# Float16 pairs for every second group of four heads in a sigmoid attention with a gated layer

## The chip, the core and the metric

One core of one Trainium2 chip runs the whole program in one launch. The metric is the device time of an execution in microseconds (us); three executions of the kernel before took 1127.08, 1126.84 and 1126.88 us, median 1126.88. Five engines work beside each other, each through its own instructions in order, and wait for one another by semaphores: TensorE (PE, with its weight loads as PEld), VectorE (DVE), ScalarE (ACT), GpSimd (POOL) and SyncE (SP), whose queue starts nearly all transfers.

## The reference

The inputs are q, k and v of 8 batches, 12 heads, 448 positions and 64 numbers a head, and three weights, all float32 by value.

```
scores = scale * np.matmul(q, k.transpose(0, 1, 3, 2)) - np.log(S)
attn = 1.0 / (1.0 + np.exp(-scores))
attn_out = np.matmul(attn, v)
x = attn_out.transpose(0, 2, 1, 3).reshape(B * S, H * D)        # 3584 x 768
gate = 1.0 / (1.0 + np.exp(-(x @ w_gate)))                      # w_gate, w_val: 768 x 1536
return gate * (x @ w_val) @ w_out                               # w_out: 1536 x 768
```

The attention has no sum over keys: each score goes through a sigmoid of its own. The weights reach the chip as 64-bit floating-point words and are converted there.

## The kernel before, in words

The program has an attention stage and a stage of layers. The layers (`product`, `unit`, `first_layers`, `c_visit`) form every product as sums of float16 pairs: a matrix is split into a high and a low float16 part, and three products (low x high, high x high, high x low) are added up in PSUM. L659 issues them all. So their operands have to be split by the chip first: `convert` does it for the weights, `split_x` for x.

**The attention stage.** Its loop (from L584) goes over 24 groups m, each of four heads of one batch (two pairs p of two heads h), and in each group over 7 beats g. A beat takes 64 keys of all four heads or, in the slots of this version, 128 keys of one pair with one mixed slot in the middle (g = 3). `scores(m, g)` forms four float32 products of 64 x 64 by 64 x 448 on four quarters of the array (L502) into one of two PSUM tiles `sc`, then ScalarE takes the sigmoid of all 896 columns (L510). Two beats later (`LAG`) `values` multiplies with v (L527) and adds up in PSUM tiles `av`. A pair of heads has two such sums, so `finish` copies one (L537) and `finish_adds` adds the other by VectorE (L544), and the result x goes to DRAM.

**Beside the beats.** After the TensorE work of a beat the loop issues a share of other work, in an order that is written out by hand; every engine keeps to that order. The generator `convert` is stepped so that its first `n_chunks` = 58 steps are spread evenly over beats 0 to 146 and the rest up to beat 168 (`BESIDE`). Two steps convert a chunk of 128 x 384 words: `begin` takes the magnitude (L214), `limit` clamps it by GpSimd (L195), `first` makes a power of two with the sign (L201, L202), `second` makes the mantissa and multiplies (L209, L210, L211); then the largest is found (L107). After four chunks the scale of a block of weights is formed from its maximum over all partitions. For that the maximum of each partition goes as `each` through TensorE (L508, into free columns of `sc`), and ScalarE copies what all partitions told (L513); this is what the text calls a telling. L126 and L120 to L123 then form the scale as powers of two (`powers`). GpSimd adds blocks (L259) and makes the high parts (L377), VectorE the low parts (L229), and SP stores them. From group 7 on the x of the first two batches is loaded back, its maxima are taken, and it is split too (L385 for the low parts).

**The start.** `load_first` brings q and k of the first pair, then v, then the second pair, then four tiles of words; `load_qk(m + 1)` loads the next group at g = 0 of the one before, in one of two buffers.

Of the kernel before, what the change touches and what calls it, by code (L numbers as in the profile page):

```python
# [20 lines left out]
P = 128  # L21
# [9 lines left out]
BESIDE = 146, 168  # L31

AHEAD, AHEAD_FF = 4, 3
# [22 lines left out]
def sigmoid_attention_glu_kernel(ctx: ExitStack, tc: tile.TileContext, qk, v, wg, wv, wo, out):  # L56
# [111 lines left out]
    class Words:  # L168
# [28 lines left out]
        def first(self):  # L197
# [3 lines left out]
            nc.vector.tensor_scalar(out=e, in0=e, scalar1=3, scalar2=0x3F800000, op0=ALU.logical_shift_left, op1=ALU.bitwise_and)  # L201
            nc.vector.scalar_tensor_tensor(out=e, in0=raw[:, :, 1], scalar=0xC0000000, in1=e, op0=ALU.bitwise_and, op1=ALU.bitwise_or)  # L202

        def second(self):

            raw, f = self.begun.pop(0)
            self.spent += 1
            m = self.pool.tile([P, CW], U32, tag="wm", name="wm", bufs=1)
            nc.vector.tensor_scalar(out=m, in0=raw[:, :, 1], scalar1=11, scalar2=0x80000000, op0=ALU.logical_shift_left, op1=ALU.bitwise_or)  # L209
            nc.vector.scalar_tensor_tensor(out=m, in0=raw[:, :, 0], scalar=21, in1=m, op0=ALU.logical_shift_right, op1=ALU.bitwise_or)  # L210
            nc.vector.scalar_tensor_tensor(out=f, in0=m, scalar=2.0 ** -31, in1=f, op0=ALU.mult, op1=ALU.mult)  # L211
# [266 lines left out]
    with tc.manual_schedule(), tc.tile_pool(name="att", bufs=2) as att, tc.tile_pool(name="sc", bufs=2, space=PSUM) as scp, \  # L478
            tc.tile_pool(name="av", bufs=1, space=PSUM) as avp:
        loads, avs, pending, adds, stores = {}, {}, [], [], []  # L480

        def load_qk(m):

            if m < B * NQ:
                loads[m] = [att.tile([P, 2, 2 * S], F32, tag="qk", name="qk")]
                nc.sync.dma_start(out=loads[m][0], in_=qk[m // NQ, m % NQ])

        def load_v(m):
            if m < B * NQ:
                loads[m].append(att.tile([P, 7, 2, D], F32, tag="v", name="v"))  # L490
                nc.sync.dma_start(out=loads[m][1], in_=v[m // NQ, m % NQ])

        def scores(m, g):


            qkt = loads[m][0]
            sc = scp.tile([P, 2, 512], F32, tag="sc", name="sc")
            for h in range(2):
                for u in range(2):
                    p = u if g == 3 else g // 4  # L500
                    k0 = S + (3 * P if g == 3 else g % 4 * P + u * HP)
                    nc.tensor.matmul(sc[halves[u], h, :S], lhsT=qkt[halves[h], p, k0:k0 + HP], rhs=qkt[halves[h], p, :S],  # L502
                                     start=True, stop=True)
            told = spreads[:1]
            for sp in told:
                spreads.remove(sp)
                for h in range(2):
                    nc.tensor.matmul(sc[:, h, S:], lhsT=sp.each, rhs=ident[:, halves[h]], start=True, stop=True)  # L508
# [556 lines left out]
```

## Time and profile before

| | us |
|---|---|
| median of three runs | 1126.88 |
| the profiled execution, as timed | 1127.14 |
| its span, first to last instruction | 1125.4 |
| first product of the layers starts at | 261.92 |
| busy in the span: PE, DVE, ACT, POOL | 1119.5, 790.4, 672.2, 496.9 |

The profile is of one execution; its granted TensorE clock is 0.999 of full speed. A row of a group has the line, the engine, the operation, the tile written and the tiles read, the shape and the count; behind the first bar the busy time in us and the mean of one in ns; behind the second the idle time of the engine ahead of these instructions and what ended it. A row in order of time begins with its start and its length in us. A row of a table of stretches has the length, then busy time and count for PE, PEld, DVE, ACT and POOL, then the granted clock, the busy share of the transfer engines and GB/s. Each float32 product shows as two weight loads and two products.

### The profile page before, as it was taken

The numbers are of one execution on the slowest core, as the hardware profiler recorded it, in microseconds if no ns is written. First come the engines' busy times: TensorE is split into PE (matmuls) and PEld (weight loads), VectorE is DVE, ScalarE is ACT, GpSimd is POOL, SyncE is SP. The second block draws the span as 40 slices with busy tenths as digits, with TensorE's granted clock in tenths as the row PEclk, the third lists the DMA queues.
The fourth block names the chain that finished last, engine by engine and source line by source line (L and its number), as shares of the span: only waits on it lengthen the run. The fifth ranks groups of instructions, "written<-read, shape, count | busy, mean of one in ns | idle before, by whom it ended". The sixth has DMA issues, their size and how long they took to land.

```text
span 1125.4 us, 20712 instructions
## 1 busy us (share of the span) xinstructions
PE 1119.5 (99%) x7269; PEld 554.4 (49%) x7269; DVE 790.4 (70%) x1318; ACT 672.2 (60%) x1265; POOL 496.9 (44%) x424
## 2 busy tenths in 40 slices
PE   9999999999999999999999999999999999999998
PEld 4444434445555555555555555555555555555554
DVE  3578989974574555667678887887348687676863
ACT  6777778876775765766565756666444444253430
POOL 0045778791252332253233443333365294572940
PEclk9999999999999999999999999999999999999999
DMA  7679979888687746753566798979756876867644
GB/s 254 233 245 326 320 251 316 302 281 303 241 274 254 254 144 213 265 163 104 151 216 207 236 355 256 322 235 256 223 167 200 252 225 206 277 199 247 190 127 140
DMA packets 174536, 265.30 MB, mean 236 GB/s; under 512 B 49248, under 2 KB 151392, under 8 KB 174432
## 3 DMA queue, kind: packets, MB, share of 16 engines
q1 hardware_dynamic: 174144, 263.80, 72.6%
q8 instruction: 57, 0.93, 0.3%
q14 instruction: 47, 0.39, 0.1%
q10 hardware_dynamic: 288, 0.18, 0.1%
HBM read 182.48 MB, written 81.43 MB: 235 GB/s over the span
## 4 chain that ended last, share of the span: by engine, by line
PE 99%; ACT 0%; DVE 0%; DVEq 0%; issue 0%
PE un L659 76%; PE av L527 11%; PE sc L502 11%; PE sc L565 0%; PE sc L508 0%; ACT a L510 0%; PE un L627 0%; DVE g L944 0%; DVEq L1060 0%; DVE bias L79 0%; DVEq L944 0%
## 5 line engine op out<-in xcount | busy, mean ns | idle before, releaser
L659 PEld LDWEIGHTS <-A 128*128 128x128 f16 x3024 | 295.5, 98 | 275.8 <-issue 0.7
L659 PE MATMUL un<-b,A 128*128 128x448 f16 x1512 | 296.6, 352 | 0.0
L659 PE MATMUL un<-b,v 128*128 128x448 f16 x1512 | 296.3, 352 | 0.0
L659 PE MATMUL un<-hh,A 128*128 128x448 f16 x1008 | 273.0, 352 | 0.0
L659 PEld LDWEIGHTS <-v 128*128 128x128 f16 x1512 | 147.8, 98 | 137.7
L510 ACT ACTIVATE a<-sc,bias 128x896 f32<-128x896 f32 x168 | 169.5, 1010 | 62.4 <-PE sc L502 54.5
L659 PE MATMUL un<-hl,A 128*128 128x448 f16 x504 | 177.6, 352 | 0.0
L527 PE MATMUL av<-a,v 64*64 64x448 f32 x1344 | 166.5, 537 | 0.0
L502 PE MATMUL sc<-qk 64*64 64x448 f32 x1344 | 165.8, 537 | 0.4 <-ACT a L510 0.4
L869 POOL TENSOR_TENSOR g<-c,g 128x448 f32<-128x448 f32 x44 | 59.1, 1344 | 184.9 <-DVE c L642 98.2
L195 POOL TENSOR_SCALAR wf<-wf 128x384 f32<-128x384 f32 x72 | 41.9, 582 | 204.3 <-ACT wf L217 131.8
L854 ACT ACTIVATE g<-c,back 128x448 f32<-128x448 f32 x72 | 48.2, 670 | 77.6 <-DVE c L642 75.1
L502 PEld LDWEIGHTS sc<-qk 64*64 64x64 f32 x1344 | 56.1, 133 | 74.7 <-issue 59.5
L642 DVE TENSOR_TENSOR c<-un,u 128x448 f32<-128x448 f32 x72 | 44.8, 622 | 66.6 <-PE un L659 58.3
L527 PEld LDWEIGHTS av<-a,v 64*64 64x64 f32 x1344 | 56.0, 133 | 68.9 <-issue 64.8
L259 POOL TENSOR_TENSOR wf<-wf 128x384 f32<-128x384 f32 x72 | 82.7, 1154 | 13.2 <-DVE whl L229 12.2
L345 POOL TENSOR_TENSOR v<-v 128x448 f32<-128x448 f32 x48 | 64.0, 1362 | 51.6 <-DVE hl L385 50.6
L345 POOL TENSOR_TENSOR b<-b 128x448 f32<-128x448 f32 x48 | 67.5, 1442 | 40.6 <-DVE hl L385 40.6
L675 ACT COPY p<-un 128x448 f32<-128x448 f32 x48 | 25.6, 533 | 57.9 <-PE un L659 57.6
L345 POOL TENSOR_TENSOR r<-r 128x448 f32<-128x448 f32 x36 | 46.5, 1306 | 24.2 <-DVE b L385 23.8
L544 DVE TENSOR_TENSOR x<-av,x 128x448 f32<-128x448 f32 x48 | 29.8, 620 | 38.8 <-ACT x L537 37.6
L104 ACT ACTIVATE junk<-g 128x448 bf16<-128x448 f32 x88 | 50.7, 576 | 7.4 <-POOL g L869 5.9
(348 smaller groups left out, 1361.2 us busy)
## 6 DMA issues: line engine op xcount, KB each, us to landing
A<-ad SPq DMA_DIRECT2D x168, 192.0 KB, 3.3
A<-oo SPq DMA_DIRECT2D x168, 192.0 KB, 2.6
qk<-qk SPq DMA_DIRECT2D x23, 896.0 KB, 5.5
h<-g SPq DMA_DIRECT2D x88, 224.0 KB, 3.4
ad<-whl SPq DMA_DIRECT2D x84, 192.0 KB, 4.1
bd<-b SPq DMA_DIRECT2D x30, 448.0 KB, 3.5
b<-bd SPq DMA_DIRECT2D x30, 448.0 KB, 5.8
v<-vv SPq DMA_DIRECT2D x24, 448.0 KB, 5.1
```

The source lines that it names most:

```text
L104: nc.scalar.activation(junk[:, :x.shape[-1]], x, AF.Abs, accum_out=to)
L195: nc.gpsimd.tensor_scalar(out=f, in0=f, scalar1=F32_MAX, scalar2=F64_ZERO, op0=ALU.min, op1=ALU.max)
L259: nc.gpsimd.tensor_tensor(out=x, in0=y, in1=z, op=op)
L345: engine.tensor_tensor(out=to, in0=x, in1=y, op=ALU.subtract)
L502: nc.tensor.matmul(sc[halves[u], h, :S], lhsT=qkt[halves[h], p, k0:k0 + HP], rhs=qkt[halves[h], p, :S], start=True, stop=True)
L510: nc.scalar.activation(a, sc[:, :, :S], AF.Sigmoid, bias=bias, scale=scale)
L527: nc.tensor.matmul(avs[key][halves[h], :S], lhsT=vt[halves[u], g, h], rhs=a[halves[u], h], start=start, stop=g == last)
L544: nc.vector.tensor_tensor(out=x, in0=other, in1=x, op=ALU.add)
L642: engine.tensor_tensor(out=to, in0=x, in1=y, op=ALU.add)
L659: nc.tensor.matmul(acc, lhsT=w, rhs=m, start=begin and i == 0, stop=i == len(terms) - 1, skip_group_check=not begin)
L854: nc.scalar.activation(gates[i], acc, AF.Sigmoid, scale=of_unit[0])
L869: nc.gpsimd.tensor_tensor(out=h, in0=acc, in1=gates[i], op=ALU.mult)
```

## The change

**Slots.** Every beat now takes 64 keys of all four heads: quarter (h, p) of the array works for head h of pair p in `scores` and in `values` alike. A pair of heads has one sum, `av` is kept twice, the adds by VectorE are gone, and ScalarE copies the two sums of a group in the second and third beat of the next (`finish_copy`).

**Float16 pairs.** In groups with odd m the scores are three rounds of four float16 products (low k x high q, high k x low q, high x high) with separate weight loads. `split_qk(m + 1)` makes the parts during group m, one step a beat: at g = 0 the largest magnitudes of q and of k in each partition (one reduction of 1792 elements, L499, and L501); behind the scores of g = 2 TensorE sums them over the partitions (four products of two columns, L545), ScalarE copies the sums behind that beat's sigmoid (L556); at g = 3 VectorE forms the powers and the two high parts (L509 to L515); at g = 4 and g = 5 the low parts of q and of k (L518). In group 0 all of this is one beat later. The powers undone go into the sigmoid as its scale. The buffer for both parts is one, that for q and k is three, and `load_qk(m + 2)` loads two groups ahead.

**Tellings** now use quarters of the array (L551) in place of the whole.

**Conversion.** `first` and `second` put sign, exponent and mantissa together by shifts and masks, three operations in place of five, also for the weights that are converted beside the layers. Its pace is 58% of the steps up to beat 77 and the rest up to beat 150; three tiles of words are loaded ahead, not four. Loading, subtracting and splitting x start up to three groups earlier.

```
-            nc.vector.tensor_scalar(out=e, in0=e, scalar1=3, scalar2=0x3F800000, op0=ALU.logical_shift_left, op1=ALU.bitwise_and)
+            nc.vector.tensor_scalar(out=e, in0=e, scalar1=3, scalar2=0x3FFFFFFF, op0=ALU.logical_shift_left, op1=ALU.bitwise_and)
...
-            m = self.pool.tile([P, CW], U32, tag="wm", name="wm", bufs=1)
-            nc.vector.tensor_scalar(out=m, in0=raw[:, :, 1], scalar1=11, scalar2=0x80000000, op0=ALU.logical_shift_left, op1=ALU.bitwise_or)
-            nc.vector.scalar_tensor_tensor(out=m, in0=raw[:, :, 0], scalar=21, in1=m, op0=ALU.logical_shift_right, op1=ALU.bitwise_or)
-            nc.vector.scalar_tensor_tensor(out=f, in0=m, scalar=2.0 ** -31, in1=f, op0=ALU.mult, op1=ALU.mult)
+            e = f.bitcast(U32)
+            nc.vector.scalar_tensor_tensor(out=e, in0=raw[:, :, 0], scalar=29, in1=e, op0=ALU.logical_shift_right, op1=ALU.bitwise_or)
...
-BESIDE = 146, 168
-AHEAD, AHEAD_FF = 4, 3
+PACE = (0, 0), (77, 0.58), (150, 1)
+AHEAD, AHEAD_FF = 3, 3
...
+        def split_qk(m):
+            if m >= B * NQ or not in_halves(m):
+                return
+            x = loads[m]
+            each = att.tile([P, 2], F32, tag="qkm", name="qkm", bufs=1)
+            told = att.tile([P, 2], BF16, tag="qkt", name="qkt", bufs=1)
+            nc.vector.tensor_reduce(out=each, in_=x.rearrange("r p t s -> r t p s"), axis=AX.XY, op=ALU.max,
+                                    apply_absolute_value=True)
+            nc.vector.tensor_scalar(out=told, in0=each, scalar1=SUM_MAX, scalar2=TINY, op0=ALU.min, op1=ALU.max)
+            yield
+            total = att.tile([P, 2, 2], F32, tag="qka", name="qka", bufs=1)
+            qk_sums.append((told, total))
+            yield
+            yield
...
+            nc.vector.tensor_tensor(out=m_, in0=total[:, 0], in1=total[:, 1], op=ALU.add)
+            powers(m_, s_, inv)
+            nc.vector.tensor_scalar(out=back, in0=inv[:, 0:1], scalar1=inv[:, 1:2], scalar2=scale, op0=ALU.mult, op1=ALU.mult)
+            hl = att.tile([P, 2, 2, 2, S], F16, tag="hl", name="hl", bufs=1)
+            parts[m] = hl, back
+            for t in range(2):
+                nc.vector.tensor_scalar(out=hl[:, 0, t], in0=x[:, :, t], scalar1=s_[:, t:t + 1], scalar2=None, op0=ALU.mult)
+            yield
+            for t in range(2):
+                nc.vector.scalar_tensor_tensor(out=hl[:, 1, t], in0=x[:, :, t], scalar=s_[:, t:t + 1], in1=hl[:, 0, t],
+                                               op0=ALU.mult, op1=ALU.subtract)
+                yield
...
+            for i, (kt, qt) in enumerate(((1, 0), (0, 1), (0, 0)) if in_halves(m) else ((None, None),)):
+                for h in range(2):
+                    for p in range(2):
+                        qs, ks_ = (x[halves[h], qt, 0, p], x[halves[h], kt, 1, p, ks]) if in_halves(m) else \
+                            (x[halves[h], p, 0], x[halves[h], p, 1, ks])
+                        nc.tensor.matmul(sc[halves[p], h, :S], lhsT=ks_, rhs=qs, start=i == 0, stop=i == 2 or not in_halves(m))
...
+            for p, queue in enumerate((nc.sync, nc.scalar)):
+                queue.dma_start(out=first[:, p, :S + P], in_=qk[0, 0][:, p, :S + P])
+            for p in range(2):
+                nc.sync.dma_start(out=first[:, p, S + P:], in_=qk[0, 0][:, p, S + P:])
+            load_qk(1)
+            load_v(0)
```

**TensorE where a group opens.** Before, around the opening of group 2 (the load of its q and k is the transfer waited for; `a` is the sigmoid's result):

```order
L527 MATMUL av<-a,v 64x448 x4
L502 MATMUL sc<-qk 64x448 [waits DMAHW3_49,Activation_49]
L502 MATMUL sc<-qk 64x448 x3
L527 MATMUL av<-a,v 64x448 x4
L502 MATMUL sc<-qk 64x448 [waits Activation_49]
```

Now, the opening of group 3, the second with float16 parts (`hl` holds them):

```order
L539 MATMUL sc<-qk 64x448 [waits Activation_49]
L539 MATMUL sc<-qk 64x448 x3
L569 MATMUL av<-a,v 64x448 x4
L539 LDWEIGHTS hl [waits DVE_49]
L539 MATMUL sc<-hl 64x448 [waits Activation_49]
L539 LDWEIGHTS hl
L539 MATMUL sc<-hl 64x448
```

The first scores of such a group wait for VectorE, and their weight loads stand as instructions of their own.

**VectorE between the beats.** Before, in the conversion (`whl` holds parts of the weights, `wm` the mantissas):

```order
L229 SCALAR_TENSOR_TENSOR whl<-wf,w00s,whl 128x384 [waits Pool_49]
L107 TENSOR_REDUCE w01c<-wf 128x1 [waits DVE_49]
L214 TENSOR_SCALAR wf<-wraw 128x384 [waits DMAHW1_49]
L201 TENSOR_SCALAR wf<-wf 128x384 [waits Pool_49]
L202 SCALAR_TENSOR_TENSOR wf<-wraw,wf 128x384 [waits DVE_49]
L229 SCALAR_TENSOR_TENSOR whl<-wf,w00s,whl 128x384 [waits Pool_49]
L209 TENSOR_SCALAR wm<-wraw 128x384
L210 SCALAR_TENSOR_TENSOR wm<-wraw,wm 128x384 [waits DVE_49]
L211 SCALAR_TENSOR_TENSOR wf<-wm,wf 128x384 [waits DVE_49]
```

Now, the parts of group 15, made during group 14, from the high parts to the second low part:

```order
L515 TENSOR_SCALAR hl<-qk,qk_2561 128x896 [waits PE_49]
L515 TENSOR_SCALAR hl<-qk,qk_2561 128x896
L518 SCALAR_TENSOR_TENSOR hl<-qk,qk_2561,hl 128x896 [waits DVE_49]
L229 SCALAR_TENSOR_TENSOR whl<-wf,w11s,whl 128x384 [waits DMAHW3_49,Pool_49]
L109 TENSOR_REDUCE w20c<-wf 128x1
L214 TENSOR_SCALAR wf<-wraw 128x384 [waits DMAHW1_49]
L203 TENSOR_SCALAR wf<-wf 128x384 [waits Pool_49]
L204 SCALAR_TENSOR_TENSOR wf<-wraw,wf 128x384 [waits DVE_49]
L518 SCALAR_TENSOR_TENSOR hl<-qk,qk_2561,hl 128x896
```

Five steps of the conversion (L203 and L204 are the former L201 and L202, L109 the former L107) stand between the two low parts. What stands there differs from group to group.

**VectorE at the start.** Before, its first work:

```order
L214 TENSOR_SCALAR wf<-wraw 128x384 [waits DMAHW5_49]
L214 TENSOR_SCALAR wf<-wraw 128x384 [waits DMAHW6_49]
L201 TENSOR_SCALAR wf<-wf 128x384 [waits Pool_49]
L202 SCALAR_TENSOR_TENSOR wf<-wraw,wf 128x384 [waits DVE_49]
L544 TENSOR_TENSOR x<-av,x 128x448 [waits Activation_49]
```

Now (`qkm` are the maxima of group 1, `qka` the sums as ScalarE copied them):

```order
L214 TENSOR_SCALAR wf<-wraw 128x384 [waits DMAHW6_49]
L499 TENSOR_REDUCE qkm<-qk 128x2 [waits DMAHW4_49]
L501 TENSOR_SCALAR qkt<-qkm 128x2 [waits DVE_49]
L509 TENSOR_TENSOR qk_341<-qka 128x2 [waits Activation_49]
```

The first magnitude of the weights, which waits for a transfer, stands ahead of the first maxima, which the fourth beat of TensorE needs.

More of the change, by code (lines that the diff above doesn't have):

```diff
@@ L488, in load_v @@
         def load_v(m):
             if m < B * NQ:
-                loads[m].append(att.tile([P, 7, 2, D], F32, tag="v", name="v"))
-                nc.sync.dma_start(out=loads[m][1], in_=v[m // NQ, m % NQ])
+                values_of[m] = att.tile([P, 7, 2, D], F32, tag="v", name="v")
+                nc.sync.dma_start(out=values_of[m], in_=v[m // NQ, m % NQ])
         def scores(m, g):
-            qkt = loads[m][0]
             sc = scp.tile([P, 2, 512], F32, tag="sc", name="sc")
[L498 to L503, printed above, removed]
@@ L504, in scores @@
-            told = spreads[:1]
+            x, ks, unit = loads[m], slice(g * HP, g * HP + HP), scale
+            if in_halves(m):
+                x, unit = parts[m]
+            for i, (kt, qt) in enumerate(((1, 0), (0, 1), (0, 0)) if in_halves(m) else ((None, None),)):
[4 more added lines that the diff above has]
+                        nc.tensor.matmul(sc[halves[p], h, :S], lhsT=ks_, rhs=qs, start=i == 0, stop=i == 2 or not in_halves(m))
@@ L505, in scores @@
+            sums = qk_sums[:1]
+            for sp, _ in sums:
+                qk_sums.pop(0)
+                for h in range(2):
+                    for u in range(2):
+                        nc.tensor.matmul(sc[halves[u], h, S:S + 2], lhsT=ones[halves[h]], rhs=sp[halves[h]], start=True, stop=True)
+            told = [] if sums else spreads[:1]
             for sp in told:
@@ L507, in scores @@
                 for h in range(2):
-                    nc.tensor.matmul(sc[:, h, S:], lhsT=sp.each, rhs=ident[:, halves[h]], start=True, stop=True)
+                    for u in range(2):
+                        nc.tensor.matmul(sc[halves[u], h, S:], lhsT=sp.each[halves[h], halves[u]], rhs=ident[halves[h], halves[h]],
+                                         start=True, stop=True)
             a = att.tile([P, 2, S], F32, tag="a", name="a", bufs=3)
-            nc.scalar.activation(a, sc[:, :, :S], AF.Sigmoid, bias=bias, scale=scale)
+            nc.scalar.activation(a, sc[:, :, :S], AF.Sigmoid, bias=bias, scale=unit)
+            for _, total in sums:
+                nc.scalar.copy(total, sc[:, :, S:S + 2])
             for sp in told:
@@ L569, in sigmoid_attention_glu_kernel @@
         warm_up(2)
+        ones = const.tile([P, HP], BF16, name="ones")
+        nc.vector.memset(ones, 1.0)
         words = Words(att, chunks(halves_of_jps[:FIRST], ()), AHEAD, 6, magnitude_vector)
@@ L609, in sigmoid_attention_glu_kernel @@
             values(*pending.pop(0))
-            finish_adds()
-        beat += 3
+        while copies:
+            finish_copy()
+        beat += 2
         finish_stores()
```

85 lines of the change are left out of this document (42 added, 43 removed).

## The prediction

> **What bounds the kernel now.** I read the page first: the busy shares and the shares of the chain that ended last.
>
> ```profile
> PE 1119.5 (99%) x7269; PEld 554.4 (49%) x7269; DVE 790.4 (70%) x1318; ACT 672.2 (60%) x1265; POOL 496.9 (44%) x424
> PE 99%; ACT 0%; DVE 0%; DVEq 0%; issue 0%
> PE un L659 76%; PE av L527 11%; PE sc L502 11%; PE sc L565 0%; PE sc L508 0%; ACT a L510 0%; PE un L627 0%; DVE g L944 0%; DVEq L1060 0%; DVE bias L79 0%; DVEq L944 0%
> ```
>
> TensorE is the chain for 99% of the span, so only its work and its new waits change the time. 76% lies in the layers behind the attention, which the change leaves as they are on TensorE. A table of stretches shows that there is nothing to win there either, though the conversion of weights that runs beside it gets shorter:
>
> ```profile
> 300.00:500.00 200.00, 200.00 (x1062) 103.56 (x1061) 123.49 (x207) 131.36 (x302) 65.64 (x58) 1.00 0.67 222
> ```
>
> TensorE is busy 200.00 of 200 us (the column behind the length), VectorE (DVE) 123.49. So the question is the attention, up to the first layer product at 261.92 us. Its chain in order of time, around one beat:
>
> ```profile
> 119.31 0.75 PE sc L502 x8
> 120.06 0.16 PE sc L508 x2
> 120.23 0.91 PE av L527 x8
> 121.14 0.75 PE sc L502 x8
> 121.89 0.75 PE av L527 x8
> 122.64 0.75 PE sc L502 x8
> ```
>
> A beat is 0.75 us of scores and 0.75 us of values, back to back (121.14 to 122.64: 1.50). Each float32 product shows as two records, so eight records are four products on four quarters of the array. A beat that also tells a maximum (L508) takes 119.31 to 121.14, which is 1.83: the full-array product between quarter-array ones costs 0.33.
>
> **The change part by part.**
>
> *The products.* In 12 of 24 groups, 84 beats, the scores become three rounds of four float16 products. No float16 product on a quarter of the array is in this trace. The nearest are the layers':
>
> ```profile
> 261.92 13.79 PE L659 MATMUL un<-b,A 128*128 128x448 f16 x72
> ```
>
> 13.79 / 72 is 0.19 us for 448 columns. With four quarters side by side, as the float32 records show them, a round takes 0.19 and the scores 0.565 in place of 0.75: 84 x 0.185 = 15.6 us gained. Bounds: it can't be below three rounds; above, if loads and products are handed over no faster than the 16 pairs of a beat now (1.50 / 16 = 0.094 a pair), 12 pairs take 1.13. I take 0.565, since waiting pairs are seen to start together: the eight loads at 6.74 quoted below share 0.33 us.
>
> *The tellings.* The eight of L508 become products on quarters. They lose the 0.33 and keep something like 0.10 (four or eight small products; from 0 to the 0.16 of the row): 2.6 - 0.8 = 1.8 gained. Twelve new sums of two columns, at the same 0.08 or so, cost 1.0. Net 0.8 gained, bounds 0 to 2.5.
>
> *The start.* Rows of the weight loads, of VectorE and of TensorE:
>
> ```profile
> 6.74 0.33 PEld L527 LDWEIGHTS av<-a,v 64*64 64x64 f32 x8 [0.42 <-DMA v<-vv]
> 8.50 0.14 PEld L502 LDWEIGHTS sc<-qk 64*64 64x64 f32 x3 [0.70 <-DMA qk<-qk]
> 9.49 0.36 DVE L214 TENSOR_SCALAR wf<-wraw 128x384 uint32<-128x384 uint32 x1 [8.41 <-DMA wraw<-wg]
> 10.46 0.36 DVE L214 TENSOR_SCALAR wf<-wraw 128x384 uint32<-128x384 uint32 x1 [0.61 <-DMA wraw<-wg]
> 14.70 0.98 PE L502 MATMUL sc<-qk 64*64 64x448 f32 x8
> ```
>
> Group 1 opens at 14.70 (its scores are the eighth set of eight records). Now the first words of weights landed at 9.49 behind 1344 KB of q, k and v, the second 384 KB took 0.97 us more. After the change 2240 KB are ahead of the first words (qk of two groups, then v): 512 KB more than the end of the second words, 1.3 us, so about 11.75. VectorE starts with those words (L214), and only then reads the maximum of group 1's q and k (a reduction of 1792 elements, 2.0 us, worked out below): told at 14.2. The fourth scores' sums wait for that; then sigmoid 1.0, copy 0.2, and the chain of 5.2 below: low parts at 21.0 and group 1 opens at 21.0 instead of 14.7. That is 6.3 later. Transfers with longer rows may be quicker: I take 6.0, bounds 4 to 7.5.
>
> *VectorE's load.* Rows of groups in the attention (mean ns behind the comma), then a stretch in order of time:
>
> ```profile
> L209 DVE TENSOR_SCALAR wm<-wraw 128x384 uint32<-128x384 uint32 x28 | 16.3, 582 | 0.0
> L211 DVE SCALAR_TENSOR_TENSOR wf<-wm,wf 128x384 f32<-128x384 uint32 x28 | 17.1, 610 | 1.0
> L202 DVE SCALAR_TENSOR_TENSOR wf<-wraw,wf 128x384 uint32<-128x384 uint32 x28 | 19.7, 702 | 0.9
> L201 DVE TENSOR_SCALAR wf<-wf 128x384 uint32<-128x384 uint32 x28 | 11.1, 398 | 0.0
> L214 DVE TENSOR_SCALAR wf<-wraw 128x384 uint32<-128x384 uint32 x28 | 10.4, 372 | 9.0 <-DMA wraw<-wg 9.0
> L229 DVE SCALAR_TENSOR_TENSOR whl<-wf,w20s,whl 128x384 f16<-128x384 f32 x7 | 6.4, 911 | 0.0
> L544 DVE TENSOR_TENSOR x<-av,x 128x448 f32<-128x448 f32 x45 | 27.9, 620 | 34.8 <-ACT x L537 33.6 <-PE sc L502 1.0
> ```
>
> ```profile
> 94.68 0.55 DVE L107 TENSOR_REDUCE w10c<-wf 128x1 f32<-128x384 f32 x1
> 95.14 0.35 DVE L214 TENSOR_SCALAR wf<-wraw 128x384 uint32<-128x384 uint32 x1
> 95.41 0.35 DVE L201 TENSOR_SCALAR wf<-wf 128x384 uint32<-128x384 uint32 x1
> 95.80 0.56 DVE L202 SCALAR_TENSOR_TENSOR wf<-wraw,wf 128x384 uint32<-128x384 uint32 x1
> 96.28 0.28 DVE L126 TENSOR_REDUCE w01m<-all 128x1 f32<-128x128 f32 x1
> 96.59 0.15 DVE L120 TENSOR_SCALAR invw<-w01m 128x1 uint32<-128x1 uint32 x1
> 96.78 0.15 DVE L121 TENSOR_SCALAR w01s<-invw 128x1 uint32<-128x1 uint32 x1
> 96.96 0.15 DVE L122 TENSOR_SCALAR w01s<-w01s 128x1 f32<-128x1 f32 x1
> 97.03 0.14 DVE L123 TENSOR_SCALAR invw<-invw 128x1 f32<-128x1 f32 x1
> ...
> 101.95 0.61 DVE L229 SCALAR_TENSOR_TENSOR whl<-wf,w01s,whl 128x384 f16<-128x384 f32 x1
> 102.48 0.55 DVE L107 TENSOR_REDUCE w10c<-wf 128x1 f32<-128x384 f32 x1
> ```
>
> Starts follow closer than durations: 0.46 behind a reduction, 0.27 behind L214, 0.39 and 0.48 behind L201 and L202, 0.53 behind L229, 0.19 for a small dependent step. The change takes away 28 x (582 + 610) ns = 33 us and the adds (28 us), and adds 12 splits. One split: the reduction is 0.55 + 1408 x 1.04 ns (one element per 1.04 ns, the 400 of L229's 530 ns over 384) = 2.0; a low part is 0.53 + 512 x 1.04 ns = 1.06; a high part of 896 elements is 0.53 if it goes as L214 (384 elements, 0.27, so 0.52 ns each), 1.0 if as L229. The small steps are 0.9. About 6.2 us, 75 in all against 61 saved. VectorE is not the bound by its sum, and its earlier deadline holds too: from one split's end to the next maximum it has some 8 to 13 us of work in 13.0.
>
> *The chain from sums to low parts.* This is where the gain goes. Rows at a telling:
>
> ```profile
> 119.13 0.93 PE L502 MATMUL sc<-qk 64*64 64x448 f32 x8
> 120.32 1.01 ACT L510 ACTIVATE a<-sc,bias 128x896 f32<-128x896 f32 x1 [0.21 <-PE sc L508]
> 121.23 0.26 ACT L513 COPY all<-sc 128x128 f32<-128x128 f32 x1
> ```
>
> The copy ends 2.36 us after the scores began. For the new sums I take 2.3, since no full-array product is between. Only then can VectorE form the powers and both parts. The sums stand in the third beat of the group before, and the split's products open the eighth: 5 x 1.50 + 0.1 = 7.6 us behind the same start, less 0.25 for loading weights and signals. That leaves 7.6 - 0.25 - 2.3 = 5.1 us. The bare chain is 0.9 + 2 x 0.53 + 1.06 + 1.14 (with its own end) = 4.15. But VectorE works in order and the conversion's steps stand inside it: in groups 3 and 5 a reduction, L214, L203, L204 (0.46 + 0.27 + 0.39 + 0.48 = 1.60); in 7 and 15 an L229 as well (2.13); in 9 one more reduction (2.66); in 11 a scale besides (3.0); in 13 only L211 (0.47); in 17 nothing; in 19, 21 and 23 1.35, 2.75 and 1.06. What exceeds 0.95 stalls TensorE, with the values and all later scores queued behind the first load: 0.65 + 0.65 + 1.2 + 1.7 + 2.1 + 0 + 1.2 + 0 + 0.4 + 1.8 + 0.1 = 9.8 us. These are undisturbed durations; beside GpSimd they are longer:
>
> ```profile
> 121.18 1.50 POOL L345 TENSOR_TENSOR xt<-u,p 128x448 f32<-128x448 f32 x1
> 121.61 1.29 DVE L209 TENSOR_SCALAR wm<-wraw 128x384 uint32<-128x384 uint32 x1
> ```
>
> ```profile
> 100.00:150.00 50.00, 50.00 (x536) 20.19 (x532) 47.17 (x92) 37.17 (x45) 35.35 (x32) 1.00 0.92 310
> ```
>
> GpSimd is busy 35 of 50 us, and L209 took 1.29 us until the subtraction beside it was over. By the means of the rows above (L202 702 against 560, L229 911 against 610, L209 582 against 350) each of four to seven such steps in a chain costs 0.1 to 0.3 more, about 0.8 a chain: the eleven stalls would be 18. I take 13, between the two, bounds 4 (if the copy comes 0.5 earlier than I think) and 18.
>
> The Trainium skill, "SBUF — State Buffer", section "Who interferes with whom", states the rule: a vector instruction in a two-port mode, or with two SBUF inputs against a GpSimd instruction that reads, and the GpSimd instruction exclude each other for a whole instruction. The 1.29 us row agrees. By the rule alone every one of the four big steps of a chain could be held, which is the second rival below.
>
> *Answers of one kind.* The adds' going frees TensorE of nothing; the copies by ScalarE fit beside a sigmoid of 1.01 in a beat of 1.32, since only two of seven beats have one. The 64-key slots keep the values at 0.75. One beat less of loading ahead (three buffers of words) is hidden by some 18 us between a load and its use. The conversion's new pace moves work from late to early and is in the groups' steps as counted. All of it costs 0; if ScalarE fell behind by a copy, some 0.3 to 0.5 a group (the 0.26 of the small copy, scaled up).
>
> *The sum.* -15.6 - 0.8 + 6.0 + 13 = +2.6 us. The profiled execution took 1127.14 us in all (span 1125.4); with the change 1129.7. The median of the runs, 1126.88, lies 0.26 below that execution, so I forecast 1129.5. A difference under 0.2% (2.25 us) can't be told from none here; +2.6 is just beyond.
>
> **The rivals.**
>
> *The chain fits (faster).* Place: the first load of every second group. The point is 15.6 + 0.8 - 6.0 = 10.4 us of stalls, 0.95 for each of eleven groups; below that the change wins. For it: the undisturbed sum, 9.8, is below the point already; GpSimd's work also loses vector steps to collide with, and VectorE's total is 14 us higher only. Against it: the steps inside the chain are in the program's order and can't move. With stalls of 4 and a start of 4 the sum is -8.4: 1118.5.
>
> *VectorE is held by GpSimd in the chain (slower by much).* Place: the two high parts, if they go in a two-port mode and meet a GpSimd step of 1 to 1.5 us, or go at one element a step (1.0 in place of 0.53). Price 0.95 for each of ten groups with no room left: +9.5 on the sum, 1139. For it: the 1.29 row; against it: L214 and L201, of the same kind, mean only 372 and 398 ns in their groups, hardly more than the undisturbed 350.
>
> *The products are bound by being handed over.* At 0.094 us a pair the scores take 1.13, a beat 1.88: 84 x 0.38 = 31.5 lost instead of 15.6 gained: 1176. For it: no row shows pairs closer in a steady run than 16 in 1.50 us. Against it: these rows are bound by the array, and nothing in them waits for the sequencer. The Trainium skill, "TensorE: Matmul & The Clock Gate", section "Wait — 56ns, not 53.3ns?", has a rule of this kind: where the hardware decoder is off, each matmul costs the sequencer about 62 ns. By it twelve products would take an estimated 0.74 us, the scores would gain next to nothing, and the sum would be about +17; no run here shows which decoder is on.
>
> **How the numbers follow.** The forecast's case (stalls of 9 to 17, start of 4 to 7.5) has 0.42 and its own range 1123.5 to 1135; half of it lies within 0.2%, half above. The chain fits: 0.34, faster. Held by GpSimd: 0.17. Handing over: 0.07. So faster 0.34, the same 0.22, slower 0.44. The range leaves out the last rival and the outermost of the first two: 1117 to 1140. It is wide because the stalls are a difference of two near numbers, the chain and its 5.1 us, taken eleven times.
>
> **What would show it.** In the profile after: scores of the second groups in rounds of 0.19 us (right) or over 0.25 (third rival). Waits of the first load of hl for VectorE, eleven times about 1.2 us, none before groups 13 and 17: if they are missing, my 5.1 us or my steps are wrong. Group 1 opening near 21 us, with TensorE waiting for VectorE's maximum at the fourth beat. High parts of 0.6 us, low ones of 1.15. The first layer product near 264.5 instead of 261.9; everything behind it as long as before (863 us). A layer stage that changes by over 1 us would make the account wrong in its premise.

## The result, and the profile after

| | before | after |
|---|---|---|
| median of four runs, us | 1126.91 | 1147.63 (1146.19 to 1148.44) |
| span of the profiled execution | 1125.4 | 1144.5 |
| opening of group 1 | 14.70 | 21.46 |
| first product of the layers | 261.92 | 281.24 |
| span behind it | 863.5 | 863.3 |

The change makes the kernel slower by 20.7 us: ratio 1.018, 95% interval 1.0168 to 1.0192. The forecast had 1129.5, with a range to 1140. The layers take what they took (863.3 us for 863.5); the loss lies ahead of them. The profile is of the execution of 1146.19 us, the fastest of the four. The page of the changed kernel, busy shares and the chain that ended last:

```profile
PE 1110.9 (97%) x7669; PEld 549.2 (48%) x7669; DVE 768.2 (67%) x1271; ACT 676.8 (59%) x1277; POOL 501.0 (44%) x424
PE 84%; DVE 11%; DMA 2%; POOL 1%; issue 1%; ACT 1%; SPq 0%; DVEq 0%; ACTq 0%; POOLq 0%
```

TensorE was 99% of the chain, and is 84% now; VectorE has 11%. What TensorE waits for up to 300 us (us in total, times, longest):

```profile
PE sc L539 <- DVE hl L518: 20.3, 10, 3.2
PE sc L545 <- DVE qkt L501: 6.3, 4, 1.9
```

The first row is the wait for the low parts, the one that the prediction costed. The second is the wait for the maximum. The first of its four times, 1.77 us at 14.28, belongs to the start as forecast; the other three, at the third beat of later groups, it had said would not come. The chain of group 3, in order of time:

```profile
35.83 0.06 ACT qka L556
35.91 0.17 DVE qk L509
...
37.00 1.19 DVE hl L515 x2
38.19 1.06 DVE hl L518
39.25 0.46 DVE w00c L109
39.71 0.27 DVE wf L214
39.98 0.28 DVE wf L203
40.28 0.74 DVE wf L204
41.02 1.07 DVE hl L518
42.14 0.76 PE sc L539 x12
```

This is the chain as it was worked out, step by step: powers, two high parts, a low part, four steps of the conversion between (1.75 us), the second low part, the opening. The scores then take 0.57 us (chain rows of a settled group) as forecast. VectorE's busy time stands behind the counts of PEld, as the third of the busy times, in these stretches:

```profile
85.00:133.00 48.00, 41.65 (x520) 18.14 (x524) 44.28 (x91) 31.96 (x40) 26.72 (x23) 0.96 0.86 302
133.00:180.00 47.00, 42.16 (x524) 17.13 (x516) 43.46 (x77) 35.62 (x44) 37.06 (x31) 0.96 0.75 252
```

VectorE is busy 44.28 of 48 and 43.46 of 47 us, while TensorE stands still for 6.35 and 4.84. A busy VectorE alone does not do that. In the kernel before it was busy 42.25 us in the first of these stretches (and 43.36 in the second), with TensorE full in both:

```profile
85.00:133.00 48.00, 48.00 (x515) 19.30 (x510) 42.25 (x90) 35.87 (x43) 25.93 (x23) 1.00 0.95 322
```

What is new is that TensorE waits, at two beats of every pair of groups, for what VectorE makes in its order. Undisturbed, two groups (a float32 one and a split one) take 19.84 us, as the kernels below show between openings. The eleven pairs of the changed kernel take 20.68, 20.68, 22.28, 24.60, 23.96, 23.04, 23.49, 19.90, 21.51, 23.94 and 23.15: together 29.0 us more than eleven times 19.84. The prediction had 13 for them.

### The profile page after: what moved, and what is told of

The parts are those of the page before. It is cut to its first block, busy times and chain, and to the rows that moved or that the text cites. A ratio compares the mean times of both kernels' runs of the same rounds, so it can differ in the third digit from the quotient of the medians.

```text
span 1144.5 us, 21414 instructions
## 1 busy us (share of the span) xinstructions
PE 1110.9 (97%) x7669; PEld 549.2 (48%) x7669; DVE 768.2 (67%) x1271; ACT 676.8 (59%) x1277; POOL 501.0 (44%) x424
## 4 chain that ended last, share of the span: by engine, by line
PE 84%; DVE 11%; DMA 2%; POOL 1%; issue 1%; ACT 1%; SPq 0%; DVEq 0%; ACTq 0%; POOLq 0%
PE un L710 75%; PE av L569 5%; PE sc L539 4%; DVE hl L518 2%; DVE hl L515 1%; DVE whl L229 1%; DVE wf L204 1%; DVE qkm L499 1%; POOL whl L377 1%; DMA wraw<-wg 1%; ACT a L554 1%; DVE wf L211 1%; DMA u<-xd 1%; DVE x0c L109 0%; DVE wf L214 0%
## 5 line engine op out<-in xcount | busy, mean ns | idle before, releaser
L569 PE MATMUL av<-a,v 64*64 64x448 f32 x1344 | 158.2, 546 | 1.1 <-DMA v<-vv 1.1
L554 ACT ACTIVATE a<-sc,bias,qkb 128x896 f32<-128x896 f32 x84 | 92.5, 1103 | 35.9 <-PE sc L539 23.5
L554 ACT ACTIVATE a<-sc,bias 128x896 f32<-128x896 f32 x84 | 84.6, 1007 | 40.9 <-PE sc L539 28.1
L259 POOL TENSOR_TENSOR wf<-wf 128x384 f32<-128x384 f32 x72 | 80.1, 1116 | 15.8 <-DVE whl L229 14.9
L539 PE MATMUL sc<-hl 64*64 64x448 f16 x1008 | 63.9, 358 | 20.3 <-DVE hl L518 20.3
L539 PE MATMUL sc<-qk 64*64 64x448 f32 x672 | 80.6, 556 | 0.6 <-DMA qk<-qk 0.6
L569 PEld LDWEIGHTS av<-a,v 64*64 64x64 f32 x1344 | 47.5, 135 | 47.2 <-issue 34.4
L693 DVE TENSOR_TENSOR c<-un,p 128x448 f32<-128x448 f32 x48 | 29.9, 623 | 52.7 <-PE un L710 48.8
L539 PEld LDWEIGHTS <-hl 64*64 64x64 f16 x1008 | 29.0, 109 | 72.2 <-issue 36.7
```

The source lines that it names most:

```text
L259: nc.gpsimd.tensor_tensor(out=x, in0=y, in1=z, op=op)
L539: nc.tensor.matmul(sc[halves[p], h, :S], lhsT=ks_, rhs=qs, start=i == 0, stop=i == 2 or not in_halves(m))
L554: nc.scalar.activation(a, sc[:, :, :S], AF.Sigmoid, bias=bias, scale=unit)
L569: nc.tensor.matmul(avs[m][p][halves[h], :S], lhsT=vt[halves[p], g, h], rhs=a[halves[p], h], start=g == 0, stop=g == 6)
L693: engine.tensor_tensor(out=to, in0=x, in1=y, op=ALU.add)
```

## The experiments

By the prediction a split has 5.1 us of room between the copy of its sums and the opening. The first four kernels take the candidates apart.

**The split in one piece.** The two `yield`s between the high and the low parts are taken out:

```
             for t in range(2):
                 nc.vector.tensor_scalar(out=hl[:, 0, t], ...)
-            yield
             for t in range(2):
                 nc.vector.scalar_tensor_tensor(out=hl[:, 1, t], ...)
-                yield
```

> The split's two high and two low parts are issued in one piece, so that none of the weight conversion's steps stands between them in VectorE's order; the steps come behind instead. Theory A (the openings are late because steps of the conversion stand inside the chain, as the prediction's sum had it): the chain falls to about 4.2 us, 4.9 beside GpSimd, below the 5.1 us of room; most of the 28.5 us lost in eleven pairs goes, 1147.6 becomes 1122 to 1130, and TensorE's waits for the low parts fall from 20.3 us (30.5 with those of its weight loads) below 8. Theory B (VectorE comes late to the whole chain, because it is behind with other work, the x work and its transfers above all, before the sums are even told): the four pairs from 85 to 180 us keep most of their 18 us, the others gain some 6: 1138 to 1143. Theory C (collisions with GpSimd inside the four big steps): hardly a change, 1144 to 1148.

1141.42 us, 6.2 less. Openings of the first pairs lie 19.84, 19.88 and 19.81 apart, so there the conversion's steps inside the chain were the whole loss. From 80 us on little is won: the pairs take 21.80, 28.85, 21.62, 21.07, 21.54, 20.94, 24.50 and 23.30. The wait has moved from the low parts (7.5 us in all) to the maximum (13.2), and one row has nearly half of it:

```profile
121.07 0.22 PE L543 MATMUL sc<-qkt,ones 64*64 64x2 bf16 x4 [6.31 <-DVE qkt L501]
```

Theory A holds for the early groups only; the time is theory B's.

**The split three beats earlier.**

```
-                if (m, g) == (0, 1) or m > 0 and g == 0:
-                    splitting = split_qk(m + 1)
+                if (m, g) == (0, 1) or m % 2 and g == 4:
+                    splitting = split_qk(m + 1 if m == 0 else m + 2)
```

> The whole split from group 3 on begins three beats earlier, at the fifth beat of the second group before it, with nothing else changed: the same work for VectorE, some 4.2 us more room in front of the opening (5.1 becomes 9.3). Theory A (the chain is longer than its room) and theory C (it is longer because of GpSimd) both expect the waits for the low parts to go but for group 1: 28.5 us less at most, 1119 to 1124, the first layer product at 253 to 257 us, and the granted clock 1.00 before the openings. Theory B (VectorE's sum of work is the bound from 85 to 180 us): it is 44.3 of 48 and 43.5 of 47 us busy there, and without TensorE's waits the same work would have to go into some 40 us; the wait moves to another place, about 9 of the 28.5 us go, 1137 to 1141.

1140.67 us, 7.0 less, as theory B had it. With 9.3 us of room the waits for low parts are gone but for 2.2 us; the maximum is waited for 14.8 us. The stretch of the longest wait, as a chain:

```profile
81.03 0.33 SPq L184
81.37 0.06 issue
81.42 5.46 DMA p<-xd
86.89 0.02 issue
86.91 0.62 DVE x0c L109
87.53 1.94 DVE qkm L499
...
106.09 0.08 DVE w10m L128
106.17 0.35 SPq L184
106.52 0.05 issue
106.57 7.24 DMA g<-xd
113.81 0.02 issue
113.83 0.62 DVE x0c L109
114.45 1.94 DVE qkm L499
...
116.71 0.22 PE sc L545 x4
```

SP issues in order. A load of words (L184) waits for VectorE to free a buffer; a load of x stands behind it; VectorE, in order too, waits for that x (L109) ahead of the maximum (L499) that TensorE needs. VectorE holds itself up, through SP. The attention ends 11.5 us earlier (269.79), but then 4.33 us are lost ahead of the layers' second set of products, on which more below.

**The x work back where it was.** Its three conditions are those of the kernel before (`g in (1, 3, 5)`, `first_x + 4`, `first_x + 7`).

> The loading of x, its maxima, differences and splits go back to the beats that they had before the change (three loads in seven beats in place of five, differences two groups later, splits three groups later); everything else is as changed. Theory B (the x work moved forward fills VectorE from 85 to 180 us, and its waits for x transfers hold the chain): the losses of the pairs opening at 109.70 and 133.66 (4.8 and 4.2 us) fall by half or more, and so do the two waits for the sums at 99.53 and 124.86; the later pairs may lose a part of it again: 1138 to 1144. Theory A (conversion steps in the chain) and theory C (GpSimd in general): the x work costs nothing wherever it is, 1146 to 1149. Slower than 1149 would mean that the move forward was a gain, because x splits beside the last groups' chains cost more.

1150.27 us: slower still, above the 1149 from which on the move forward counts as a gain; theory B's 1138 to 1144 did not come. TensorE waits for the maximum 0.7 us at the start and nowhere else, and in 62 to 133 us VectorE idles 9.1 us ahead of L509 (2.9 in the changed kernel), so it is no longer late there. Yet the openings stay where they were (109.55 and 133.91 us for 109.70 and 133.66). Part of the reason is in VectorE's rows behind the sums of group 9:

```profile
101.27 0.16 DVE L509 TENSOR_TENSOR qk<-qka 128x2 f32<-128x2 f32 x1 [3.83 <-ACT qka L556]
...
105.81 0.61 DVE L109 TENSOR_REDUCE x0c<-u 128x1 f32<-128x448 f32 x1
106.33 3.16 DVE L518 SCALAR_TENSOR_TENSOR hl<-qk,qk,hl 128x896 f16<-128x896 f32 x2
109.41 0.93 DVE L229 SCALAR_TENSOR_TENSOR whl<-wf,w01s,whl 128x384 f16<-128x384 f32 x1
```

The chain alone takes 8.3 us (101.27 to 109.55) for 5.1: a maximum of x stands in it as well, and two low parts take 3.16 in place of 2.2. So there are two limits, one behind the other: the chain's room, and VectorE being late to the maximum. These two do not account for the time alone. In the pair up to 109.55 TensorE waits 2.71 us, where it had waited 1.19 and 3.16, and 1.6 us are lost instead because the clock is halved from 86 to 90 us, which it was not before; the pair up to 133.91 has 2.60 of wait for the low parts in place of 1.92 for the maximum. Up to 290 us half clock costs 12.7 us in this execution (the slowest of its four) and 4.8 in that of the changed kernel. The x splits, now beside the last groups, cost 5.82 us at the last opening.

**No split at all.** `in_halves` returns False.

> No group is split: the scores of all groups are float32 products, while the slots of 64 keys, the tellings on quarters, the copies by ScalarE, the shorter conversion, its pace and the earlier x work stay as changed. By the prediction's account these cost nothing and the tellings give back 1.8 us: 1125.1 (1124 to 1126). If the rest of the change is itself a part of the loss (the x work, the order of the first loads, three buffers of words in place of four), it is over 1128; the whole difference to 1147.6 is then split between the two.

1126.89 us, ratio 0.9998 (0.9989 to 1.0008), between the two cases expected. The rest of the change together is neutral, so the 20.7 us belong to the splits. It is neutral as a sum: group 1 opens at 18.96 us even so, 4.3 later than before, since v comes behind two groups of q and k (a wait of 2.25 us) and half clock from 11 to 15 us takes 1.7 in this execution; the layers start at 263.08, only 1.2 later. VectorE's load without splits:

```profile
85.00:133.00 48.00, 48.00 (x524) 19.53 (x520) 36.81 (x80) 36.45 (x45) 32.46 (x29) 1.00 0.95 341
133.00:180.00 47.00, 47.00 (x508) 19.16 (x504) 30.40 (x50) 37.57 (x46) 37.80 (x31) 1.00 0.84 279
```

Here a pair takes 21.07 us (14 beats of 1.505), so VectorE has 36.81 / 48 x 21.07 = 16.2 us of work a pair, then 13.6. A split is 6.6 us by its rows (2.0 for L499, 1.4 for two L515, 2.2 for two L518, 1.0 for the small ones of 0.2). 22.8 and 20.2 us do not go into 19.84. These busy times hold what GpSimd's work adds to VectorE's steps.

The next four ask how strict this limit is, and try two smaller suspects.

**Seven splits.** `in_halves`: m in (3, 5, 7, 17, 19, 21, 23), begun three beats early.

> Begun three beats earlier as in the kernel with the early split, but only groups 3, 5, 7, 17, 19, 21 and 23 are split; 1, 9, 11, 13 and 15 stay float32. Theory V (VectorE's sum of work per pair of groups is the bound from 85 to 180 us: 36.8 us of 48 without splits, 16.2 a pair, plus 6.6 for a split, against a pair of 19.8): the seven groups that stand where VectorE has room give their 1.3 us each and make no wait: 1126.9 of the kernel without splits less 9.1 is 1117.8 (1117 to 1120). Theory T (a split is late wherever it is, through transfers or queues that come late): some 1 us is lost at each of the seven, 1122 to 1128.

In the attention theory V fits: TensorE waits for the maximum 1.7 us in all, is busy 48.00 of 48 and 47.00 of 47, and the layers' first product comes at 254.29, 8.8 earlier than without splits (9.1 expected). Some of the 8.8 is luck: group 1, float32 in both, opens 2.2 earlier (16.75 for 18.96), with v there sooner and the clock full. The time is 1126.9, as without splits; this is in theory T's range, but not for its reason. The gain goes at the hand-over:

```profile
260.66 1.56 PE L710 MATMUL un<-b,A 128*128 128x448 f16 x6 [4.49 <-ACT x L579]
```

ScalarE's last copy of x waits for a buffer whose store stands in SP's queue behind the last stores of weights and eight loads of operands (in the chain SP issues them from 250.58 to 255.18 us, then come 4.63 of the store). Behind this wait half clock takes another 1.7.

**The maxima of x on ScalarE**, six loads behind their transfers (`load_x(0, new_x)` in place of `load_x(0, new_x, max_abs)`, and a distance of 6 for the two of `LAG`), with all twelve splits early.

> The early split in all twelve groups, but the twelve maxima of x are taken off VectorE: ScalarE sums the absolute values instead (another measure for the same power of two), and six loads behind the transfer in place of two, so that it does not wait for it. Theory V: 6.4 us of reductions and the 2.8 us that VectorE waits for x in 62 to 133 us leave it, and the waits for the sums in 85 to 133 (6.9 us the longest) shrink by about as much: 1140.7 becomes 1132 to 1135. Theory S (the in-order queue of SP and the transfers of q and k set the pace there): no change, 1139 to 1142. If ScalarE becomes the bound (twelve steps of some 0.6 us more beside the sigmoids) it is over 1142.

1135.78 us, 4.9 less than the early split and close to theory V. The long pair falls from 29.66 to 21.45; later ones (23.17, 21.82, 25.04) don't.

**Group 1 in float32**, the other splits early (`m % 2 == 1 and m > 1`).

> The early split, and group 1 left in float32: the start alone is undone. The opening of group 1 moved from 14.70 to 21.46 us; seven beats of 0.185 are lost again: 5.4 us. Theory 'terms add' (the prediction's sum): 1140.7 becomes 1135.3 (1134.5 to 1136). Theory V in a strict form (VectorE is behind from the first groups on and sets the time of everything up to the layers): TensorE only waits the longer later, 1138 to 1141.

1138.41 us, 2.3 less, at the lower end of the strict form of theory V; the terms do not add. Group 1 opens at 17.82 in place of 21.21, both at full clock. So the split is 3.4 us of the late start and the order of the first loads, which the kernel without splits has too, the other 3.1 (17.82 for 14.70). Less the 1.3 that its products save, the split of group 1 costs 2.1, not 5.4: group 3 opens at 38.92 for 41.05. In the two profiled executions 0.9 of this is left at the layers' first product (268.87 for 269.79), with 1.3 us more of half clock on the way.

**The wait filled.** Eight products of a constant ahead of three openings:

```
+            if g == 0 and m in (9, 13, 23):
+                warm_up(2)
```

> The changed kernel with eight float32 products of a constant (1.5 us, into scores that nothing reads) in TensorE's order ahead of the openings of groups 9, 13 and 23, where it waits 3.16, 3.03 and 3.08 us: the waits shrink by 1.5 each, the openings stay where they are. Theory G (the granted clock falls because TensorE stands still for more than some 2 to 3 us, and the rows after the openings are longer for that: 1.33 and 1.55 in place of 0.57 and 0.75 at 156.70, 1.17, 1.49 and 1.11 at 268.69): the clock stays at 1.00 in 125 to 130, 155 to 160 and 265 to 275 us, the rows are 0.57 and 0.75, and 3 to 5 us go: 1142.5 to 1145. Theory N (the slow rows have another cause, such as the loads of hl): the rows stay and so does the time, 1146 to 1149.

1147.37 us: unchanged, which is theory N's time. Yet the clock did what theory G says where the wait was filled. The granted clock is the third number from the right, first in the changed kernel, then here:

```profile
155.00:160.00 5.00, 3.30 (x36) 1.47 (x40) 4.97 (x8) 1.25 (x2) 2.10 (x3) 0.66 0.57 188
```

```profile
155.00:160.00 5.00, 3.59 (x60) 1.57 (x56) 4.96 (x8) 2.10 (x3) 2.10 (x3) 1.00 0.58 192
```

From 265 to 270 us it is 1.00 in place of 0.89. The rows behind the opening at 156.90 are 0.76, 0.78 and 0.57 in place of 1.33, 1.55. But the clock fell elsewhere instead, behind the waits at 84.76 and 179.41: summed over 1 us stretches up to 290 us, busy time times the missing clock is 4.8 us in the changed kernel and 4.9 here.

**Six loads' distance, the maxima on VectorE** (the edit of the distance alone).

> The early split in all twelve groups (1140.67), and the maxima of x stay on VectorE, but each stands six loads behind its transfer in place of two. Theory D (what costs most from 85 to 133 us is that VectorE, which works in order, waits for transfers of x that stand in SP's queue behind loads of words, which wait for VectorE: 5.46 and 7.24 us of the chain there): the pair that opens at 101.12 and 130.78 falls from 29.7 to 21.5 to 23 us, as where ScalarE took the sums, and the time to 1132 to 1135. Theory V (the sum of VectorE's work): its 6.4 us of maxima are still there, only the 2.8 us of listed waits go: 1137 to 1139.

1139.43 us, nearest to theory V. The long pair falls to 25.06, which is 4.6 us of the 7 that theory D wanted, but the pair from group 15 to 17 takes 25.04 where it had taken 21.65.

**The conversion's casts on ScalarE** (`scaled` for `scaled_gpsimd` in `convert`).

> The kernel with the six loads' distance, and the conversion's casts to float16 moved from GpSimd to ScalarE (some 50 of 1.25 us in the attention; 0.5 us each on ScalarE). Theory C (VectorE's steps are lengthened by GpSimd's work beside them, 7.5 us in 85 to 133 and 13.2 in 133 to 180 over the shortest of their kind): about half of that goes, the pairs between 131 and 197 us (20.6, 24.2, 21.6) come near 20, and the time is 4 to 6 us below the kernel with GpSimd's casts. If it is not the lengthening but ScalarE's own queue that VectorE then waits for, or the sigmoids stand behind casts, no gain or a loss of up to 5 us.

1139.66 us: no gain. GpSimd's busy time in 133 to 180 us falls from 38.25 to 22.23 and VectorE's from 45.43 to 41.15, so the collisions were real; but TensorE now waits 8.5 us for sigmoids that stand behind casts. How much the collisions alone cost the changed kernel stays open.

The last four follow the gain that is lost at the hand-over.

**The operands' loads behind the store** (seven splits; `load_operands(RING)` at g == 5 of the last group, for g == 0).

> The kernel with seven split groups (1126.9), whose attention ended 8.8 us earlier than without splits (254.29 against 263.08 us) and which then waited 4.5 us for ScalarE's last copy, whose buffer waited for a store of x that stood in SP's queue behind eight loads of the layers' operands and the last stores of weights. Here those loads are issued five beats later, behind that store. Theory Q (SP's order alone makes that wait): the wait goes and the layers start near 254.5 at full clock: 1121 (1120 to 1123). Theory E (the end of the weight conversion, at 250.6 us, sets the start of the layers whatever the order): TensorE then waits for operands instead, 1125 to 1128.

1132.45 us, slower by 5.5: both missed, E had the mechanism. The loads now stand behind the last stores of weights as well, and the conversion ends near 261.6 us:

```profile
264.82 1.68 PE L710 MATMUL un<-b,A 128*128 128x448 f16 x4 [8.31 <-DMA A<-ad]
```

**Four buffers for the copies of x** (seven splits; `bufs=4` for `bufs=3`, the loads where they were).

> Seven split groups begun early (1126.9), with four buffers for the copies of x in place of three, so that ScalarE's last copy waits for a store of an earlier group; the loads of the operands are where they were. Theory Q (that buffer alone holds the layers): they start at 254.3 without the wait of 4.5 us and at full clock: 1121 to 1123. Theory E (the weights' conversion, which ends near 255 us on GpSimd, sets the start): TensorE waits for operands of the layers instead, and the time is 1125 to 1128.

1123.42 us, ratio 0.9968 (0.9957 to 0.998): faster than both kernels, and theory Q's mechanism, just above its range. The layers start at 256.31 without a wait and at full clock. That is 2.0 later than with three buffers, since group 1 opens 2.0 later in this execution (18.77 for 16.75); against the kernel without splits, whose group 1 opens at 18.96, seven splits give 6.8 us.

**The conversion ahead** (the same; `PACE` (77, 0.62), (140, 1), all steps by beat 160).

> As the kernel with four buffers, and the weights' conversion runs ahead: the first seven groups of words end at beat 140 in place of 150, all steps at 160 in place of 168. Theory E: the conversion's end moves some 8 beats, 11 us, forward and the gain of the attention is kept: 1118 to 1121. Theory Q expects 1121 to 1123 here too. If VectorE has no room for the faster conversion between 85 and 220 us (37.4 of 48 and 33.7 of 47 us busy), waits for the sums come back: over 1124.

1128.19 us: the last of the cases expected. The wait for the maximum is back, where the conversion's end now meets a split (4.92 us at 239.74).

**Two more splits, groups 11 and 13** (on the faster conversion, maxima of x at six loads' distance).

> As the kernel with the faster conversion, with groups 11 and 13 split as well and the maxima of x six loads behind their transfers. Theory V (a split fits where VectorE's busy time and 6.6 us stay below the pair): 37.4 + 6.6 of 46.7 and 33.7 + 6.6 of 45.7 us fit in sum, by little, and more conversion comes on top: 0 to 2.6 us below the kernel with seven splits if they fit; 2 to 5 us above it if VectorE's order brings waits of 1 to 3 us back.

1138.6 us, 10.4 more, twice what the worse case expected. Waits for a telling (L552, 2.46 us at 130.74) and for the copy of the sums (3.85 at 142.86) come in, and in 133 to 180 us TensorE is busy 43.15 of 47. VectorE is busy only 38.04 of 47 there. Room by the sum of busy times, 33.7 and a split's 6.6 in 45.7 us, was not room in VectorE's order.

## Why the prediction was wrong

The direction was right. Of the rivals, the chain did not fit and the hand-over of products cost nothing; VectorE was held by GpSimd, but mostly in the low parts and the small steps, and not at every opening. The size was off by 18 us. Term by term, up to the layers (19.3 us later):

| term | predicted | measured |
|---|---|---|
| products, 84 beats | -15.6 | -15.5 (0.57 for 0.75) |
| tellings and sums | -0.8 | +0.1 with small waits not listed (the remainder) |
| start | +6.0 | +6.8 |
| wait for low parts behind the first | +13 | +18.6 (nine listed waits) |
| wait for the maximum behind the first | 0 | +4.5 |
| half clock behind waits | 0 | +4.8 |

**Right.** The products, the rows of the chain where nothing disturbs them, its room (in group 3 the opening at 42.14 less a wait of 0.67, less 0.25, less the copy's end at 35.89: 5.3 for 5.1), and the opening of group 1 (21.46 for 21.0) with the way to it: the words landed at 11.73 (11.75 forecast) and the sums began at 14.28 (maximum told at 14.2).

**The stalls, group by group.** The prediction's undisturbed sum beside the listed waits for low parts, in us:

| group | 3 | 5 | 7 | 9 | 11 | 13 | 15 | 17 | 19 | 21 | 23 |
|---|---|---|---|---|---|---|---|---|---|---|---|
| predicted | 0.65 | 0.65 | 1.2 | 1.7 | 2.1 | 0 | 1.2 | 0 | 0.4 | 1.8 | 0.1 |
| waited | 0.67 | 0.61 | 2.27 | 3.16 | 0 | 3.03 | 1.98 | 0 | 1.53 | 2.28 | 3.08 |

Groups 3, 5 and 17 came as worked out. Group 11's chain took 7.35 us and shows no listed wait, since TensorE ran at half clock meanwhile (1.7 us) and came to the opening 7.4 us behind the copy. Group 23's began 2.06 us after the copy of its sums, since VectorE was behind with other work and had itself waited 0.29 and 1.15 us for GpSimd's high parts. Group 13's had one conversion step inside, as foreseen, and took 8.27 us: beside GpSimd its small steps took 2.07 in place of 1.0, L211 1.27 in place of 0.47, the low parts 3.33 in place of 2.12. Rows of the chain up to the opening, then GpSimd's at the same time:

```profile
152.05 1.27 DVE wf L211
153.32 3.33 DVE hl L518 x2
156.70 1.33 PE sc L539 x12
```

```profile
151.54 1.36 POOL L259 TENSOR_TENSOR wf<-wf 128x384 f32<-128x384 f32 x1
152.89 1.54 POOL L377 TENSOR_SCALAR whl<-wf,w10s 128x384 f16<-128x384 f32 x1
```

With GpSimd the prediction had 18 for all stalls, then took 13. That 18.6 came is in part luck, since groups 11, 13 and 23 are off by 2 to 3 us each.

**The step that failed** first is in "VectorE's load": "VectorE is not the bound by its sum, and its earlier deadline holds too: from one split's end to the next maximum it has some 8 to 13 us of work in 13.0". The sum was made over the whole attention, 75 us in against 61 out, where it looks harmless. By stages it is 22.8 us a pair against 19.84 from 85 to 133 us; and VectorE's waits for transfers, which the sum of steps leaves out, come on top, since the work behind them waits as well. What the runs showed in its place are 4.5 us of waits for the maximum, put at 0, and the late beginnings of the chains of groups 9 and 23. Two experiments bear it out: the early split removed the chain and left this limit, and with the five groups taken out of the splits as well it all but went. Neither parts VectorE's own work from what GpSimd adds to it. With the 4.8 us of half clock, also put at 0 (below), the 4.5 carry the time out of the range: by these terms it would have been some 1138 without both.

**"All of it costs 0"**, said of the x work, failed with it. Without splits it does cost nothing; with them it put twelve maxima, and waits for transfers, where VectorE had no slack. Moving it back uncovered the chain, and more of the half clock.

**Steps lengthened by GpSimd** were put at 0.8 us a chain. Two low parts together took 1.06 + 1.07 in group 3 and 3.1 to 3.3 in groups 7, 9 and 13: 1.0 to 1.2 in these alone, and in group 13 as much again in the small steps. The Trainium skill, "SBUF — State Buffer", section "Who interferes with whom", has for this an exclusive lock between a vector instruction with two SBUF inputs, as L518 is, and a GpSimd instruction that reads. The rows agree for L518; the durations of L515 (0.68 at the median, 1.19 at the most) say that it seldom struck there.

**The clock** was in no term. Stretches of 1 us around the wait of 1.92 us at 124.86:

```profile
124.00:125.00 1.00, 0.14 (x8) 0.14 (x11) 0.89 (x3) 0.00 (x0) 0.28 (x1) 1.00 0.91 318
125.00:126.00 1.00, 1.00 (x16) 0.45 (x16) 0.83 (x2) 0.83 (x1) 0.00 (x0) 0.77 0.79 305
126.00:127.00 1.00, 1.00 (x11) 0.36 (x8) 0.64 (x5) 0.66 (x3) 0.00 (x0) 0.50 0.92 238
127.00:128.00 1.00, 1.00 (x8) 0.28 (x4) 0.96 (x5) 0.33 (x1) 0.00 (x0) 0.50 0.77 233
128.00:129.00 1.00, 1.00 (x12) 0.50 (x8) 1.00 (x3) 0.67 (x1) 0.00 (x0) 0.52 0.93 355
129.00:130.00 1.00, 1.00 (x19) 0.39 (x16) 1.00 (x4) 0.03 (x1) 0.00 (x0) 1.00 0.15 49
```

The clock is halved after the work has begun again, for some 3.4 us, and 1.7 us go on top of the 1.92.

What stays open: how the losses from 85 to 200 us divide between VectorE's own work, its waits in order and GpSimd's collisions (taking the maxima of x off it gave 4.9, the longer distance alone 1.2, the casts moved 0, all with the early split, and each time a part came back at a later pair or in another wait); at which waits the clock falls; and the few us that the layers of the best kernel lose at their start: 866.6 us behind the first product for 863.1 without splits, with two waits of 1.3 us among them.

## What to carry to other kernels

Work that is added to an engine off the critical path has to be summed by stages, against the new and shorter length of each stage, with the engine's waits in order counted as work; a sum over the whole program hid the loss here. Such a sum is a condition and no promise: nine splits fitted by it and cost 10.4 us. Where a chain has too little room, ask what is late next before you cost its removal: here the chain and the engine's backlog hid each other, and only taking five of the splits out, beginning the rest early and adding a buffer gave a gain (1123.42). A stage that ends earlier needs its hand-over looked at: 4.5 us of wait and 1.7 of half clock stood behind one buffer. And before two profiled executions are compared, compare their clocks: one spell of half clock cost 1.5 us or more here.

## What the runs showed of the hardware

Waits shorter than the clock's half-rate stretch can set it off, and not every wait does: 1.92 us at 124.86 did, 3.16 us at 109.70 did not. The Trainium skill, "TensorE: Matmul & The Clock Gate", section "Part 1: The HAM clock gate (the "warmup" mystery)", tells of a free-running window of about 3.4 us; the 3.4 us of half clock and the dependence on the moment agree; that it takes "≥1 idle window" does not, since TensorE was busy for part of any 3.4 us around 124. Of the ten listed waits of over 1.5 us three set it off.

Four float16 products of 64 x 64 by 64 x 448 on four quarters take 0.19 us with loads of their own, as twelve did in 0.57: no hand-over limit showed at this rate.
